# Last pair of a fused FFT convolution and spectral mixer: ten rooms for Z, W and a second block of Z read at other ticks

## The chip, the cores and the metric

One core of one Trainium2 chip. The metric is the device time of one execution in microseconds. Engines are named as in the profile: PE (matmul), PEld (its weight loads), DVE, ACT, POOL and SP. POOL and SP also issue DMAs, each on a queue of its own; each takes its instructions in order, so an instruction that waits holds up all that follow it on that engine.

## The reference

Two layers over x (8 batches, 5696 positions, 128 channels): a long convolution with h by FFT, and a spectral mixer on its result.

```python
def _attn_ref(x, h):
    B, S, D = x.shape
    L = 2 * S
    Xf = np.fft.rfft(x, n=L, axis=1)
    Hf = np.fft.rfft(h, n=L, axis=0)
    return np.fft.irfft(Xf * Hf[None], n=L, axis=1)[:, :S, :]

def _moe_ref(x, w_r, w_i, w_ch):          # n_modes = 64
    X = np.fft.rfft(x, axis=1)
    Xr, Xi = X.real[:, :n_modes], X.imag[:, :n_modes]
    Yr = einsum('bmd,mde->bme', Xr, w_r) - einsum('bmd,mde->bme', Xi, w_i)
    Yi = einsum('bmd,mde->bme', Xr, w_i) + einsum('bmd,mde->bme', Xi, w_r)
    y = np.fft.irfft(Yr + 1j * Yi, n=S, axis=1)       # other modes 0
    u = x + y
    return u + np.maximum(u @ w_ch, 0.0)
```

## The kernel before

The transform of length 11392 is done as matmuls in steps, on two batches (a pair, g = 0 to 3) at a time. For each pair:

- **First step** (`a_tile`): 32 tiles bring `Xin` through `F` into `As`.
- **Ticks** (`tick(g_, t)`): 90 frequency classes are taken four at a time, in 23 ticks (NT = 23) and 3 more to drain the pipeline. Tick t does the second transform step for its classes (`As` with `M`), the products with the filter `Hs` on DVE (tile `U`, three buffers, token `("u", t % 3)`), two ticks later the first inverse step (`U` with `Wc`), whose result ACT evicts as block s = t - 2 of Z into a room (`Zs`, `Zt`), and SP writes to the scratch `zscr` in DRAM. One tick after that PE multiplies the block with `G`, which gathers the 64 modes that the mixer needs.

A room may be filled again when its block has been written to `zscr` and read by PE. Rooms 0 to 5 are `Zs`; rooms 6 to 9 (`Zt`) lie in memory behind `G`. The last pair uses 8 rooms (`NZS`), so that block s goes into room s % 8. The memory of rooms 8 and 9 is used for `Id`, the identity of the transposes, and for `Y`, the mixer's result. `ZY` names the tokens of rooms 8 and 9, `ZX` those of rooms 6 and 7.

After the last pair's ticks comes the **output stage**: PE starts inverse sums of pair 0 (`u_z`), mixes the modes with `W` (64 times two matmuls), the result is evicted as `Y`, transposed on PE against `Id` (line 785), evicted as `C`, and then every output tile (`u_tile`) is the sum of `ZT` blocks times `S4a` and `S4b` and of `C` times `IBs`. `ZT0` to `ZT4` are five buffers for blocks of Z read back from `zscr` (16 positions of a pair each, four blocks to a pair), in two parts, a and b. When a block's tiles are done, SP loads a later block into the buffer. `o_tile` does the last matmul, with `w_ch`, and SP writes the output.

What the output stage needs is read during the last pair's ticks, by POOL, from a table by tick (`early`), each with a wait (`pace`) for that tick's product on DVE: `W` in four pieces, `S4a`, `S4b`, `IBs`, `ZT` blocks (`load_zt`) and memsets of the unused partitions of part b (`clear_zt`). Such a load may start when the memory that it takes is free: `W` lies over `Xin`, `S4b` over the first part of `As`, ZT buffers over `As`, `Hs`, `M` and `G`. `SLACK` is a further wait, for the first 15 blocks (0 to 14) of the last pair to be written to `zscr`. After the loop follow `load_wi` (two loads of 32 KB) and the remaining ZT blocks, without `pace`.

A recorder puts down every operation with what it reads and writes, and derives the waits; an operation with `after=` waits for the writers and readers of the tokens named. The semaphores of DMAs come from rings: the ring "z" of Z's writes has 8, and a DMA waits for the one that had its semaphore before.

Of the kernel before, what the change touches and what calls it, by code (L numbers as in the profile page):

```python
# [4 lines left out]
P = 128  # L5
# [118 lines left out]
def bass_long_conv_fft__then__afno_spectral_mix_kernel(nc, x, h, moe_w_r, moe_w_i, moe_w_ch, out):  # L124
# [8 lines left out]
    NP = B // 2  # L133
    KT = 4
    NT = (NK + KT - 1) // KT
# [15 lines left out]
    c, s = np.cos(th), np.sin(th)  # L151
# [35 lines left out]
    def const(name, a):  # L187
        return nc.inline_tensor(np.ascontiguousarray(a.astype(np.float16)), name=name)
# [3 lines left out]
    c_w = const("cW", np.concatenate([w1, w2, np.eye(P)], axis=1))  # L192
# [5 lines left out]
    zs = nc.dram_tensor("zscr", [NP * NK * P, 2 * D], F16, kind="Internal")  # L198
# [7 lines left out]
    def at(name, cols, dt, off):  # L206
        return nc.alloc_sbuf_tensor_at(name, [P, cols], dt, offset=off)

    def take(nbytes):
        off = (cur[0] + 31) // 32 * 32  # L210
        cur[0] = off + nbytes
        assert cur[0] <= end, (cur[0], end)
        return off
# [10 lines left out]
    a_h = take(2 * HW * 2)  # L224
# [2 lines left out]
    g_sb = at("G", GW, F16, a_g)  # L227
    ah_sb = at("Ah", HW, F16, a_g)
    NU, NXS, NZ, NZX = 3, 2, 6, 10
    NZS = [NZ] + [NZX] * (NP - 2) + [8]  # L230
    NZL = NZS[-1]
    a_st = take((2 * NU + NXS + NZ) * 2048)
    h_in = at("Hin", J * D, F16, a_st)
    DH = D // 2
# [19 lines left out]
    NC = 5  # L254
    ZP = ZB * 2 * D
    a_h2, a_xt = a_h + HW * 2, a_x + 4 * S + 2 * B * P
    a_as1, a_m2 = a_as + 2 * S, a_m + 4 * S
    zt_off = [(a_as1, a_as1 + 2 * ZP), (a_as1 + 4 * ZP, a_as1 + 6 * ZP), (a_h, a_h2), (a_h + 2 * ZP, a_h2 + 2 * ZP),
              (a_m2, a_g)]
    assert 2 * S + 8 * ZP <= AW * 2  # L260
    zt = [[at(f"ZT{i}{'ab'[p_]}", ZP, F16, zt_off[i][p_]) for p_ in range(2)] for i in range(NC)]
# [18 lines left out]
    id_sb = at("Id", P, F16, r_off[1])  # L280
# [9 lines left out]
        return bass.AP(ps, p0 * 4096 + bank * 512 + off, [[4096, n]] + [list(d) for d in dims])  # L290

    R = Recorder(nc)
    for name, n in (("c", 16), ("x", 26), ("z", 8), ("w", 16), ("t", 10), ("s", 8), ("o", 12), ("p", 16), ("q", 10)):
        R.ring(name, n)

    def bank(i):
        return ("bank", i)
# [3 lines left out]
    def evac(dst, src, reads, writes, scale=None, eng=None, after=()):  # L301
        e = eng
        if e is None:
            turn[0] ^= 1
            e = "scalar" if turn[0] else "vector"
        if e == "scalar":
            if scale is None:
                R.add(e, lambda h_: h_.copy(dst, src), reads, writes, after=after)  # L308
            else:
                R.add(e, lambda h_: h_.activation(dst, src, COPY, scale=scale), reads, writes, after=after)  # L310
        elif scale is None:
            R.add(e, lambda h_: h_.tensor_copy(dst, src), reads, writes, after=after)  # L312
        else:
            R.add(e, lambda h_: h_.tensor_scalar_mul(dst, src, scale), reads, writes, after=after)  # L314

    def dma(eng, dst, src, ring, reads=(), writes=(), after=()):
        R.add(eng, lambda h_: h_.dma_start(dst, src), reads, writes, ring=ring, after=after)  # L317
# [6 lines left out]
    def once(key, toks):  # L324
        if key in first:
            return []
        first[key] = 1
        return list(toks)
# [3 lines left out]
    def turns(name, items):  # L332
        i = ring2.get(name, 0)
        ring2[name] = i + 1
        return items[i % len(items)]
# [87 lines left out]
    for j in range(16):  # L423
        t = turns("h", [0, 2, 4])
# [11 lines left out]
        if j % 2:  # L436
            i = j // 2 % 2 * XC + j // 4
# [4 lines left out]
    AST = [("as", j) for j in range(33)]  # L442
# [40 lines left out]
    def load_w(i):  # L483
        w = 2 * M * D // 4
        dma("gpsimd", w_sb[:, i * w:(i + 1) * w], bass.AP(wd, i * w, [[2 * M * D, P], [1, w]]),
            "p", WD, [("w", i)] + (XIN if i == 0 else []), after=pace)

    H_ALL = [("h", t, 0) for t in range(NT)] + [("h", t, 1, p0) for t in range(NT) for p0 in (0, J)]
    U_ALL = [("u", i) for i in range(NU)] + [("xs", i) for i in range(NXS)] + \
            [("zs", i, b) for i in range(NZ) for b in range(2)]  # L490
    M_ALL = [("m", i) for i in range(MP)]
    G_ALL = [("g", i) for i in range(NG)]
    WT = [("w", i) for i in range(4)]
    ZY = [("zs", i, b) for i in range(NZL, NZX) for b in range(2)]
    ZX = [("zs", i, b) for i in range(NZ, NZL) for b in range(2)]
    zt_old = [(AST, AST), (AST, AST), (H_ALL, H_ALL), (H_ALL, H_ALL), (M_ALL[3:6], G_ALL)]

    def load_zt(i, eng="sync", more=()):
        g_, c_ = divmod(i, J // ZB)
        for part, (p0, r0, n) in enumerate(((0, 0, P), (PB, P, RB))):  # L500
            old = list(once(("zt", i % NC, part), zt_old[i % NC][part])) + list(more) + pace
            dma(eng, bass.AP(zt[i % NC][part], p0 * ZP, [[ZP, n], [1, ZP]]),
                bass.AP(zs, (g_ * 2 * NK + r0) * J * 256 + c_ * ZB * 256, [[J * 256, n], [1, ZP]]),
                "q" if eng == "gpsimd" else "t", [("zd", g_, s_) for s_ in range(NT)], [("zt", i % NC, part)], after=old)

    def clear_zt(i):
        z32 = zt[i][1][0:PB, :].bitcast(U32)
        R.add("gpsimd", lambda e: e.memset(z32, 0), (), [("zt0", i)], after=list(zt_old[i][1]) + pace)

    def load_ib():  # L510
        dma("gpsimd", ib_sb[:, 0:SH], c_ib.ap(), "p", (), [("ib", 0)], after=M_ALL[0:2] + pace)
# [10 lines left out]
    def load_s4(part):  # L522
        n = PB + RB if part else P
        dma("gpsimd", s4_sb[part][0:n, 0:SH], bass.AP(c_s4, part * SH, [[2 * SH, n], [1, SH]]), "p", (),
            [("s4", part, 0)], after=pace + (AST if part else M_ALL[1:4]))

    V, A = "vector", "scalar"
    border = {NT - 1: [(0, 0, V)], NT: [(1, 2, V), (2, 0, V)], NT + 1: [(3, 2, A), (4, 0, V)], NT + 2: [(5, 2, V)]}
    early = {0: lambda: load_id(), 1: lambda: load_w(0), 3: lambda: load_w(1), 6: lambda: load_w(2), 8: lambda: load_w(3),
             12: lambda: load_s4(1), 16: lambda: load_s4(0),  # L530
             14: lambda: clear_zt(0),
             15: lambda: load_zt(0, "gpsimd"),
             NT - 2: lambda: (load_ib(), load_zt(1, "gpsimd", SLACK), load_zt(2, "gpsimd"), clear_zt(1), clear_zt(2))}
    pace = []
    SLACK = [("zd", NP - 1, s_) for s_ in range(NT - NZL)]

    def load_id():
        dma("gpsimd", id_sb[:, :], bass.AP(c_w, 2 * P, [[3 * P, P], [1, P]]), "p", (), [("id",)], after=ZY)

    def load_wi():  # L540
        dma("gpsimd", wi_sb[:, P:2 * P], bass.AP(c_w, 2 * P, [[3 * P, P], [1, P]]), "p", (), [("i16",)], after=M_ALL[5:6])
# [2 lines left out]
    def keep(n, b0):  # L544
        for i in range(n):
            mm(pv(b0 + i % 2, 0, [[1, 2 * NK]]), f1_sb[:, 0:P], f1_sb[:, :], True, True, [("f1",)], [bank(b0 + i % 2)])
# [66 lines left out]
    def zroom(g_, s_):  # L613
        return (s_ - 2 * NZ) % NZX if g_ == 0 and s_ >= 2 * NZ else s_ % NZS[g_]

# [69 lines left out]
            filter_tick((j - 11) // 3, [h_, h_ + 1])  # L685
    keep(16, turns("s", FOUR))
    for g_ in range(NP):
        for t in range(NT + LM):
            tick(g_, t)
            if g_ == 0 and t < 2:  # L690
                keep(8, 4)
            assert g_ + 1 < NP or not wp
            if g_ == NP - 1 and t in early:
                pace[:] = [("u", min(t, NT - 1) % NU)]
                early[t]()
        evac(bass.AP(xt, 2 * g_ * XTW + M, [[B * XTW, P], [XTW, 2], [1, P]]), pv(MB, 0, [[P, 2], [1, P]]),
             [bank(MB)], [("xt", g_)], 1.0 / 64, eng="scalar", after=[("ag", k) for k in range(NS + 2 * XN, NK)])
        evac(bass.AP(xt, 2 * g_ * XTW, [[B * XTW, P], [XTW, 2], [1, M]]), pv(MB, M, [[P, 2], [1, M]]),
             [bank(MB)], [("xtn", g_)], -1.0 / 64, eng="vector" if g_ + 1 == NP else "scalar", after=[("ag", k) for k in range(NS + 2 * XN, NK)])
        if g_ + 1 < NP:  # L700
            for j in range(6, 32):
                a_tile(j, [(4, 6, 0, 2)[(j - 7) % 4] if j > 6 else 0], "both" if j == 31 else V if j % 2 else A)
                if j == 31:
                    keep(8, 6)
                if wp and j % 2 == 1:
                    dst, src_, ring, tok = wp.pop(0)
                    dma("gpsimd", dst, src_, ring, (), [tok], after=[("as", j)])
# [1 line left out]

    pace[:] = []  # L710
    load_wi()
    for i in range(3, NC):
        load_zt(i, "gpsimd")
        clear_zt(i)

# [63 lines left out]
    for hb in range(2):  # L779
        evac(bass.AP(y_sb, hb * 32 * B, [[2 * M * B, P], [B, 32], [M * B, 2], [1, B]]),  # L780
             pv(6 + hb, 0, [[2 * B, 32], [B, 2], [1, B]]), [bank(6 + hb)], [("y", hb)], eng="vector" if hb else "scalar",
             after=ZY)
    for b in range(B):
        bk = 6 + b // 4
        R.add("tensor", lambda e, b=b, bk=bk: e.transpose(
# [10 lines left out]
    o_cur = [0]  # L796
    o8_old = [H_ALL] * 2 + [U_ALL] + [G_ALL + ZX] * 2 + [WT] * 2
    o_old = [H_ALL] * 2 + [M_ALL[5:6], U_ALL + [("f1",)]]
# [49 lines left out]
    for g_ in range(NP):  # L848
        last = g_ == NP - 1
        order = [(c_, b) for b in range(2) for c_ in range(NCH)] if last else [(c_, b) for c_ in range(NCH) for b in range(2)]  # L850
        for n, (c_, b) in enumerate(order):
            i = NCH * g_ + c_
# [44 lines left out]
```

## Time and profile before

| | |
|---|---|
| median of 3 runs | 393.89 us (393.86 to 394.1) |
| the profiled execution | 392.87 us, of it the span of the trace 390.6 us |
| PE | 364.1 us busy, 93% of the span |
| PEld, DVE, ACT | 72%, 77%, 80% |
| POOL | 22% |
| granted TensorE clock, mean | 0.982 |
| DMA | 103.94 MB, mean 266 GB/s |
| last pair's ticks | about 221 to 263 us |
| output stage | about 263 us to the end |

Busy shares are averages over stages with different limits; matmuls overlap, so a busy PE is not PE at its peak. The chain of waits follows back from the last instruction to what released each step. A DMA's time to landing runs from its issue to its last byte's arrival. Waits for several semaphores are put down to the one that came last.

### The profile page before, as it was taken

Reading aid. Unit: us, or ns where it says so; the run is one execution under the profiler, and the core shown is the slowest. Engines: PE = TensorE matmul, PEld = TensorE weight load, DVE = VectorE, ACT = ScalarE, POOL = GpSimd, SP = SyncE. Lnnn points to the kernel's source line nnn. Section 1 sums busy time; section 2 is a strip of 40 time slices with the busy share of each in tenths; the row PEclk is TensorE's granted clock in tenths of the full one; section 3 lists DMA queues with packets and bytes.
Section 4 is the critical chain, followed back from the end, with each engine's and each line's share of the span. In section 5 each row is a group of like instructions: output and inputs, shape, how many; then the busy total and the mean of one; then the engine's idle time right before and its main releaser. Section 6 shows DMA issues by size and latency. Waiting matters only on the chain.

```text
span 390.6 us, 12485 instructions
## 1 busy us (share of the span) xinstructions
PE 364.1 (93%) x5346; PEld 281.3 (72%) x5346; DVE 301.9 (77%) x346; ACT 311.2 (80%) x489; POOL 85.6 (22%) x134
## 2 busy tenths in 40 slices
PE   7799899998989999999989899989989999999992
PEld 7698766665866667856657666658878988988871
DVE  3369889987998998989998988754437767677784
ACT  8289689997989997899997899984447676777783
POOL 8600022210643210823213210319200000000000
PEclk9899999999999999999999999996999999999998
DMA  7998569998899995999995689999999999998766
GB/s 146 178 283 337 138 126 297 274 251 251 92 135 201 238 268 169 127 136 231 245 261 111 64 264 351 298 354 379 406 388 393 414 407 412 410 399 356 305 274 273
DMA packets 87090, 103.94 MB, mean 266 GB/s; under 512 B 22824, under 2 KB 72616, under 8 KB 83564
## 3 DMA queue, kind: packets, MB, share of 16 engines
q1 hardware_dynamic: 62523, 67.73, 49.7%
q0 software_dynamic: 24512, 35.43, 43.6%
q8 instruction: 42, 0.69, 0.7%
q14 instruction: 13, 0.10, 0.1%
HBM read 70.61 MB, written 51.12 MB: 312 GB/s over the span
## 4 chain that ended last, share of the span: by engine, by line
PE 63%; DMA 15%; DVE 8%; ACT 6%; issue 3%; POOL 3%; SPq 0%; POOLq 0%; DVEq 0%
PE ps L320 63%; DMA ZT4b<-zscr 4%; DMA zscr<-Zt 3%; DMA Hs<-Hs 3%; DMA Hin<-in_h_dram 3%; DMA Xt<-in_x_dram 2%; DVE As L314 2%; DVE U L599 2%; ACT As L310 2%; DVE U L607 1%; DVE Xin L361 1%; ACT UT L308 1%; ACT Zs L308 1%; DVE Hs L312 1%; ACT Xs L308 1%
## 5 line engine op out<-in xcount | busy, mean ns | idle before, releaser
L607 DVE TENSOR_TENSOR U<-Xs,Hs 128x2048 f16<-128x2048 f16 (+1 forms) x73 | 86.9, 1192 | 15.1 <-ACT Xs L308 11.0
L320 PE MATMUL ps<-U,Wc 128*128 128x512 f16 (+1 forms) x368 | 94.0, 376 | 1.3 <-DVE U L607 0.8
L308 ACT CAST Xs<-ps 128x1024 f16<-128x1024 f32 (+1 forms) x77 | 74.7, 974 | 11.9 <-PE ps L320 6.8
L308 ACT CAST Zs<-ps 128x512 f16<-128x512 f32 (+1 forms) x134 | 70.6, 595 | 2.7 <-PE ps L320 2.4
L832 DVE TENSOR_TENSOR O<-ps,R 128x512 f32<-128x512 f32 x81 | 52.5, 685 | 19.8 <-ACT R L831 12.5
L831 ACT ACTIVATE R<-ps 128x512 f32<-128x512 f32 x96 | 50.9, 572 | 16.3 <-PE ps L320 15.8
L314 DVE TENSOR_SCALAR As<-ps 128x720 f16<-128x720 f32 x70 | 57.7, 884 | 5.4 <-PE ps L320 4.8
L320 PE MATMUL ps<-F,Xin 128*128 128x180 f16 x512 | 53.7, 249 | 3.6 <-DVE Xin L361 2.3
L320 PE MATMUL ps<-As,M 64*128 64x128 f16 x1440 | 50.5, 217 | 3.5 <-DVE U L599 2.9
L320 PEld LDWEIGHTS ps<-F,Xin 128*128 128x128 f16 x512 | 44.4, 155 | 12.1 <-DVE Xin L361 2.8
L320 PE MATMUL ps<-WI,UT 128*128 128x256 f16 x360 | 51.8, 279 | 0.5 <-DVE O L832 0.4
L320 PEld LDWEIGHTS ps<-U,Wc 128*128 128x128 f16 x368 | 28.7, 97 | 30.3 <-ACT Zs L308 4.4
L310 ACT ACTIVATE As<-ps 128x720 f16<-128x720 f32 (+1 forms) x61 | 45.7, 770 | 5.7 <-PE ps L320 4.3
L317 POOL DMA_DIRECT2D Xt<-in_x_dram x48 | 26.0, 546 | 101.0 <-PE ps L320 97.1
L320 PEld LDWEIGHTS ps<-As,M 64*128 64x128 f16 x1440 | 40.6, 94 | 9.9 <-DVE U L599 3.6
L308 ACT CAST UT<-ps 128x712 f16<-128x712 f32 x40 | 30.0, 752 | 18.7 <-PE ps L320 17.7
L320 PEld LDWEIGHTS ps<-WI,UT 128*128 128x128 f16 x360 | 39.3, 152 | 4.2 <-issue 1.9
L320 PE MATMUL ps<-IBs,C 128*128 128x356 f16 x128 | 40.5, 326 | 0.6
L320 PEld LDWEIGHTS ps<-G,Zs 128*128 128x128 f16 x524 | 26.6, 96 | 14.9 <-ACT Zs L308 2.2
L607 DVE TENSOR_TENSOR U<-ps,Hs 128x2048 f16<-128x2048 f32 x15 | 34.3, 2283 | 0.0
L320 PE MATMUL ps<-G,Zs 128*128 128x128 f16 (+2 forms) x524 | 33.0, 192 | 0.1
L312 DVE CAST UT<-ps 128x712 f16<-128x712 f32 x24 | 21.4, 890 | 11.0 <-PE ps L320 11.0
(87 smaller groups left out, 509.8 us busy)
## 6 DMA issues: line engine op xcount, KB each, us to landing
out_dram<-O SPq DMA_DIRECT2D x39, 512.0 KB, 8.7
zscr<-Zs SPq DMA_DIRECT2D x64, 256.0 KB, 7.4
Xt<-in_x_dram POOLq DMA_DIRECT2D x24, 320.0 KB, 7.3
zscr<-Zt SPq DMA_DIRECT2D x24, 256.0 KB, 7.3
W<-wscr POOLq DMA_DIRECT2D x4, 1024.0 KB, 9.1
M<-cM POOLq DMA_DIRECT2D x5, 720.0 KB, 20.6
ZT0a<-zscr SPq DMA_DIRECT2D x3, 1024.0 KB, 13.1
Hs<-Hs SPq DMA_DIRECT2D x44, 64.0 KB, 6.3
```

Source lines behind the costliest of these rows:

```text
L308: R.add(e, lambda h_: h_.copy(dst, src), reads, writes, after=after)
L310: R.add(e, lambda h_: h_.activation(dst, src, COPY, scale=scale), reads, writes, after=after)
L312: R.add(e, lambda h_: h_.tensor_copy(dst, src), reads, writes, after=after)
L314: R.add(e, lambda h_: h_.tensor_scalar_mul(dst, src, scale), reads, writes, after=after)
L317: R.add(eng, lambda h_: h_.dma_start(dst, src), reads, writes, ring=ring, after=after)
L320: R.add("tensor", lambda h_: h_.matmul(o, l, r, start=st, stop=sp), reads, writes)
L361: R.add("vector", lambda e: e.tensor_copy(bass.AP(x_sb, i * XN * XS, [[XW, NQ], [XS, XN], [1, D]]), src), list(toks) + XZ, [("xin", i)])
L599: R.add("vector", lambda e, b=b, s_=s_: e.tensor_tensor(bass.AP(u_s[i], b * 512, [[2048, P], [1024, 2], [1, n * D]]), s_, hv, MULT), [tok, ...
L607: R.add("vector", lambda e: e.tensor_tensor(uv, src, hv, MULT), bk + [("h", t, 0), ("h", t, 1, 0), ("h", t, 1, J)], [("u", i)])
L831: R.add("scalar", lambda e: e.activation(rv, src_r, RELU), bk, [("r", i % NR)], after=once(("r", i % NR), G_ALL + XTT + [("y", 0), ("y", 1 ...
L832: R.add("vector", lambda e: e.tensor_tensor(ov, src_u, rv, ADD), bk + [("r", i % NR)], [key + (h_,)], after=once(key, old))
```

## The change

In the last pair Z gets ten rooms, as in the pairs before it, and the ring "z" ten semaphores. `ZX` now names rooms 6 to 9; `ZY` is gone. `W`'s first two pieces are issued ahead of the last pair's first tick, without `pace`; the other two at ticks 3 and 5 instead of 6 and 8, `S4b` at 8 instead of 12, `IBs` at 18 instead of 21. `ZT0` now lies over the first part of `Hs` and is read at tick 11 instead of 15; `ZT1` takes `ZT0`'s former place over `As` and is read at tick 15; at tick 21 `ZT2` and `ZT3` are read instead of `ZT1` and `ZT2`; only `ZT4` is left for after the loop. `Id` is loaded by SP at tick 25, after the last write of Z, instead of by POOL at tick 0; it and `Y`'s evictions now wait for rooms 6 to 9.

```diff
-    NZS = [NZ] + [NZX] * (NP - 2) + [8]
-    NZL = NZS[-1]
+    NZS = [NZ] + [NZX] * (NP - 1)
...
-    zt_off = [(a_as1, a_as1 + 2 * ZP), (a_as1 + 4 * ZP, a_as1 + 6 * ZP), (a_h, a_h2), (a_h + 2 * ZP, a_h2 + 2 * ZP),
+    zt_off = [(a_h, a_h2), (a_as1, a_as1 + 2 * ZP), (a_as1 + 4 * ZP, a_as1 + 6 * ZP), (a_h + 2 * ZP, a_h2 + 2 * ZP),
               (a_m2, a_g)]
...
-... ("z", 8), ...
+... ("z", 10), ...
...
-    ZY = [("zs", i, b) for i in range(NZL, NZX) for b in range(2)]
-    ZX = [("zs", i, b) for i in range(NZ, NZL) for b in range(2)]
-    zt_old = [(AST, AST), (AST, AST), (H_ALL, H_ALL), (H_ALL, H_ALL), (M_ALL[3:6], G_ALL)]
+    ZX = [("zs", i, b) for i in range(NZ, NZX) for b in range(2)]
+    zt_old = [(H_ALL, H_ALL), (AST, AST), (AST, AST), (H_ALL, H_ALL), (M_ALL[3:6], G_ALL)]
...
-    early = {0: lambda: load_id(), 1: lambda: load_w(0), 3: lambda: load_w(1), 6: lambda: load_w(2), 8: lambda: load_w(3),
-             12: lambda: load_s4(1), 16: lambda: load_s4(0),
-             14: lambda: clear_zt(0),
-             15: lambda: load_zt(0, "gpsimd"),
-             NT - 2: lambda: (load_ib(), load_zt(1, "gpsimd", SLACK), load_zt(2, "gpsimd"), clear_zt(1), clear_zt(2))}
+    early = {3: lambda: load_w(2), 5: lambda: load_w(3), 8: lambda: load_s4(1),
+             10: lambda: clear_zt(0),
+             11: lambda: load_zt(0, "gpsimd"),
+             14: lambda: clear_zt(1),
+             15: lambda: load_zt(1, "gpsimd"),
+             16: lambda: load_s4(0),
+             18: lambda: load_ib(),
+             NT - 2: lambda: (load_zt(2, "gpsimd", SLACK), load_zt(3, "gpsimd"), clear_zt(2), clear_zt(3)),
+             NT + 2: lambda: load_id()}
     pace = []
-    SLACK = [("zd", NP - 1, s_) for s_ in range(NT - NZL)]
+    SLACK = [("zd", NP - 1, s_) for s_ in range(NT - 8)]

     def load_id():
-        dma("gpsimd", id_sb[:, :], bass.AP(c_w, 2 * P, [[3 * P, P], [1, P]]), "p", (), [("id",)], after=ZY)
+        dma("sync", id_sb[:, :], bass.AP(c_w, 2 * P, [[3 * P, P], [1, P]]), "c", (), [("id",)], after=ZX)
...
     for g_ in range(NP):
+        if g_ == NP - 1:
+            load_w(0)
+            load_w(1)
         for t in range(NT + LM):
             tick(g_, t)
...
-    for i in range(3, NC):
+    for i in range(4, NC):
         load_zt(i, "gpsimd")
         clear_zt(i)
...
         evac(bass.AP(y_sb, ...), ..., [("y", hb)], eng="vector" if hb else "scalar",
-             after=ZY)
+             after=ZX)
```

More of the change, by code (lines that the diff above doesn't have):

```diff
@@ L292, in bass_long_conv_fft__then__afno_spectral_mix_kernel @@
     R = Recorder(nc)
-    for name, n in (("c", 16), ("x", 26), ("z", 8), ("w", 16), ("t", 10), ("s", 8), ("o", 12), ("p", 16), ("q", 10)):
+    for name, n in (("c", 16), ("x", 26), ("z", 10), ("w", 16), ("t", 10), ("s", 8), ("o", 12), ("p", 16), ("q", 10)):
         R.ring(name, n)
```

## The prediction

> **What bounds the kernel now.** I read the page's chain first, then the chain of waits from 218 to 305 us (the last pair's ticks and the start of the output stage), then the timelines of PE, ACT and DVE there, and last the DMA issues in narrow windows. Blocks of Z are numbered 0 to 22 by their tick in the last pair.
>
> ```profile
> PE 63%; DMA 15%; DVE 8%; ACT 6%; issue 3%; POOL 3%; SPq 0%; POOLq 0%; DVEq 0%
> ```
>
> PE holds the end; DMA holds it in a few places. Two of them lie in the stretch that the change touches (columns: start us, us, what):
>
> ```profile
> 223.63 20.23 PE ps L320 x318
> ...
> 250.16 11.91 DMA zscr<-Zt
> ...
> 267.02 1.74 POOLq L105
> 268.77 1.01 POOL WI L317 x2
> ...
> 273.48 15.12 DMA ZT4b<-zscr
> 288.59 0.05 issue
> 288.64 12.47 PE ps L320 x182
> ```
>
> Block 14 is written from 250.16 and lands at 262.07. POOL waits for it (SLACK), issues four Z loads, clears and WI, and the last, ZT4b, lands at 288.59, where PE goes on. What PE itself lost is less than the chain's DMA shares. The timeline of PE (start, us, engine, line, idle before in brackets):
>
> ```profile
> 262.86 0.58 PE L320 MATMUL ps<-G,Zt 128*128 128x4 f16 x4 [0.91 <-ACT Zt L308]
> ...
> 269.84 1.05 PE L785 MATMUL ps<-Id,Y 128*128 128x128 f16 x8 [0.23 <-issue]
> ...
> 288.64 0.21 PE L320 MATMUL ps<-S4b,ZT4b 84*128 84x89 f16 x1 [1.83 <-DMA ZT4b<-zscr]
> ```
>
> The first gap, 0.91 us, is block 22 waiting for its Z room (8 rooms: that of block 14). The last, 1.83 us, is ZT4b. Between them stand the transposes of Y with Id at 269.84, which waited for nothing but work on PE, ACT and DVE.
>
> The third thing to see is how slowly Z's writes land. Three windows of DMA issues: block 13, alone at 249 us; block 19, issued at 259.27; blocks 21 and 22 beside POOL's Z loads (KB each, us from issue to landing).
>
> ```profile
> zscr<-Zs SPq DMA_DIRECT2D x1, 256.0 KB, 5.1
> ```
>
> ```profile
> zscr<-Zs SPq DMA_DIRECT2D x1, 256.0 KB, 8.4
> ```
>
> ```profile
> ZT1a<-zscr POOLq DMA_DIRECT2D x1, 1024.0 KB, 9.7
> ...
> zscr<-Zs SPq DMA_DIRECT2D x1, 256.0 KB, 17.6
> zscr<-Zt SPq DMA_DIRECT2D x1, 128.0 KB, 20.1
> ```
>
> POOL moved 1024 KB in 9.7 us while SP needed 20.1 us for 128 KB issued at 264.31: it landed at 284.4. The trace's packet records show why: from 254 to 258 us POOL's queue moved 187 packets of 5.9 and 8.2 KB, and SP's 237 of 512 B. They take turns packet by packet, so SP runs at a tenth of its speed (59 packets per us; 1231 in the two us from 260, when POOL's queue was nearly empty). Whatever stands on SP's queue behind Z's writes crawls while POOL reads Z.
>
> **The change, part by part.** The sum is made against the profiled execution, 392.87 us (span 390.6 and 2.27 around it); the median, 393.89, is 1.0 more, which I add at the end.
>
> *Ten rooms, ring z of ten.* Block 22 then takes block 12's room; block 12 was issued at 247.3 and landed by 253.1. The 0.91 us goes. In pairs 1 and 2 the ring of 8 made no PE wait, so nothing comes there.
>
> *W's first pieces ahead of the ticks.* The last wscr piece landed at 220.74, so W0 goes at about 221.3 in place of 225.28, W1 at 221.8 in place of 228.43. DMA stood still from 222 to 226 (0 GB/s by windows), so this costs nothing and moves 2 MB out of the ticks. W is used from 264.4 and landed by 246.0: no gain by itself. W2, W3 and S4b follow two to four ticks sooner, likewise unneeded so early; they fill what W0 and W1 left, so at 250 us the queues stand about as before (from 226 to 252 us POOL moved 4.7 MB; now about 4.8: W2 and W3 2.1, S4b 0.5, a Z block 1.5, the rest of W1 0.7). The POOL memset of 1.8 us moves too; beside one at 247.3 DVE's product took 2.29 us against 2.28 elsewhere: nothing.
>
> *Z blocks.* ZT0 at tick 11 (about 242.9), ZT1 at tick 15 (249.9, where ZT0 was), S4a behind it, IBs at tick 18 (254.5 instead of 259.62), ZT2 and ZT3 after SLACK, ZT4 after the loop. Behind SLACK stand 3 blocks of 1440 KB in place of 4. While POOL alone has the engines' time it moves 0.35 MB/us (packet records of 253 to 258), so 4.2 us for each block of 1.47 MB. Even if the first starts at 266.5 (below), three end near 279 and ZT4b lands near 280, against 286.6 when PE wants it: the 1.83 us goes too. Sum so far: -0.91 - 1.83 = -2.74.
>
> *Id and Y.* This is the part that decides. Rooms 8 and 9 were free in the last pair, so Id was read at 216.44 (4.5 us) and Y's evictions waited for PE alone. With ten rooms, rooms 6 to 9 hold blocks 16 to 19, and both Id's load and Y's evictions now wait until all four are written to zscr. Block 19 landed at 267.65; Y's evictions ran at 266.81 (ACT) and 269.05 (DVE), with behind them the evictions of C and U. That alone costs 0 to 2 us if block 19 lands as before. But it lands later if anything: ZT1, S4a and IBs (2908 KB) lie on POOL's queue from 250 to 261, where ZT0 and S4a were 2174 KB. Block 14 starves until they are through, so SLACK opens at 262 to 264.2 (736 KB at 0.35 is 2.1 us), and blocks 15 to 19 have only the time until ZT2's first packet, about 2.3 us later, undisturbed.
>
> Id is issued by SP after that wait, and on its queue behind blocks 20, 21 and 22. PE stops at the transposes, in order, until Id lands; ACT and DVE have C's evictions and IBs' reflection behind them; on SP stand the reloads of ZT0 and the later blocks, which wait for the first output tiles anyway. Bounds for the landing: at the best 267.65 + 4.5 (the Id row) = 272.1; at the worst block 22's own landing of before, 284.4, shortened by one Z block of POOL's (4.2), lengthened by SLACK's 2.1 less the missing IBs' 2.1 behind it, plus half of the 4.0 us that block 22 took after block 21 (Id has 128 packets, it 256): 282.2. The WI rows, 32 KB of the same form in POOL's queue, took 9.1 and 8.9 us; from 267.65 that is 276.7, with nothing of Z ahead. I take 278.0: block 22 with POOL's queue shorter is the nearest row, but less of Z is left when ZT2 starts, as IBs no longer runs from 262 to 266.
>
> Transposes at 278.0 in place of 269.84: +8.16. After them the work is the same, and ZT4b no longer stops it: -1.83 (the 0.91 lies before the wait and is swallowed). Net +6.3, 399.2 in the profile, 400.2 as median. PE's clock: 0.50 from 268 to 274 in the windows, after the thin work from 262. The new wait is longer than that, so the clock is half when work resumes; before, PE worked some 4.5 us of half clock from the transposes on. I put the difference at 0, with 1.5 us either way.
>
> The Trainium skill (TensorE: Matmul & The Clock Gate, "The HAM clock gate") says that the clock halves after an idle window of about 3.4 us and comes back after one busy window; the two 3.4-us windows of half clock here agree. By it the resumed work could lose up to 1.7 us per window, which is inside the 1.5 either way.
>
> **Rivals.**
> *Not slower.* SP's queue empties before ZT2 starts, Id lands early. It decides at 269.84 + 1.83 = 271.7, where the wait eats what ZT4b gives: a landing over 0.8 us earlier makes the kernel faster, down to 392.87 - 2.74 + 1.02 = 391.2 when nobody waits. For it: SP moved 600 packets per us at 260 to 262, so 3 us undisturbed carry 3.5 blocks. Against: block 19 itself landed at 267.65, and 4.5 us more is too late already.
> The Trainium skill (DMA: Bandwidth & Descriptors, "Queues, rings and completion order") would speak for this rival: queues take turns by packets of some 9 to 17 descriptors, so a turn of SP's would carry as much as one of POOL's and Z's writes would not starve. The trace disagrees: 232 against 237 packets, 128 KB in 20.1 us.
>
> *Starved to the end.* If block 14 is through before tick 21, SLACK opens at once, ZT2 and ZT3 follow IBs without a gap, and blocks 15 to 19 starve too; Y waits for block 19 and Id for POOL's last packet, 282 to 284: +12.2 to +14.2, less 1.83, that is 404 to 406.
>
> *A short wait.* Id at 272.5 to 274: 394.7 to 396.
>
> *The change does not reach its aim:* ZT4b late all the same. Then PE has waited for Id long before, and it costs nothing more; only under the first rival would it take back up to 1.8.
>
> **How the numbers follow.** Forecast (Id between 274 and 282, 396 to 404) 0.53; starved to the end 0.15; short wait 0.10; not slower (Id before 272.5) 0.22, of which 0.05 within 0.8 us of 393.89 (0.2%, about what a measurement of this kernel tells from no change) and 0.17 faster. Slower: 0.53 + 0.15 + 0.10 = 0.78. The range takes in most of the first rival and the lower half of the starved case: 391.5 to 405. The forecast's own range is 396 to 404.
>
> **What would show it.** Right: in the chain, a DMA Id<-cW of SP's some 8 to 12 us long; the transposes of L785 idle for 6 to 11 us before them; Y's evictions released by a zscr write; no gap at the last G,Zt or Zs product near 262; ZT4b released by nothing. W0 issued near 221. Wrong: transposes before 271.7; or PE idle within the ticks, which would mean that rooms still ran out.

## The result and the profile after

| | before | after |
|---|---|---|
| median | 393.14 us (388.19 to 394.1, 6 runs) | 401.47 us (399.8 to 402.03, 6 runs) |
| profiled execution, span | 392.87 us, 390.6 us | 401.64 us, 399.5 us |
| transposes of Y start | 269.84 us | 280.43 us |
| granted TensorE clock, mean | 0.982 | 0.964 |

The ratio is 1.025, with a 95% interval from 1.0207 to 1.0293: slower. A ratio leaves out runs that lie over 1.5% above the fastest of their kernel, so it can differ from that of the medians.

The page's chain, as shares of the span: DMA has fallen from 15% to 11%, PE has risen by six points.

```profile
PE 69%; DMA 11%; DVE 8%; ACT 6%; issue 3%; POOL 1%; SPq 0%; DVEq 0%; POOLq 0%
```

Read by shares alone that looks better. The chain of waits in the last pair shows what has gone and what has come (start us, us, what):

```profile
222.90 33.33 PE ps L319 x524
...
258.94 17.39 DMA zscr<-Zt
276.33 0.02 issue
276.35 3.94 DMA Id<-cW
280.30 0.14 issue
280.43 1.05 PE ps L790 x8
281.48 28.56 PE ps L319 x432
```

The chain now stays on PE for 33 us of the ticks, and PE's timeline has no gap of over 0.2 us from 222.9 us to the wait for `Id`, so the room's wait is gone. It stays on PE for 28.6 us after the transposes, through the first use of ZT4b at 297.56: that wait is gone too (ZT4b landed at 278.4). Between the two stands a new piece: the write of block 19, issued at 258.94, lands at 276.33, only then SP issues Id, and Id lands at 280.30. On PE it is one gap (idle in brackets):

```profile
280.43 1.05 PE L790 MATMUL ps<-Id,Y 128*128 128x128 f16 x8 [12.67 <-DMA Id<-cW]
```

The waits from 255 to 300 us show that Y's two evictions stood for the same reason, ACT's and DVE's (us in total, times, longest):

```profile
PE ps L790 <- DMA Id<-cW: 12.7, 1, 12.7
ACT Y L307 <- DMA zscr<-Zt: 11.8, 1, 11.8
DVE Y L311 <- DMA zscr<-Zt: 10.9, 1, 10.9
```

The sum nearly closes. The transposes stand 10.59 us later, and without ZT4b's wait what follows should be 1.83 us shorter, together 8.76. The spans differ by 8.91, so what follows is 1.69 shorter, 0.14 less than that. The profiled executions, some 2 us longer than their spans, differ by 401.64 - 392.87 = 8.77; that this meets 8.76 is partly chance.

### The profile page after: what moved, and what is told of

Same layout as the page of the kernel before. It is cut to its first block, busy times and chain, and to the rows that moved or that the text cites. A ratio compares the mean times of both kernels' runs of the same rounds, so it can differ in the third digit from the quotient of the medians.

```text
span 399.5 us, 12468 instructions
## 1 busy us (share of the span) xinstructions
PE 362.9 (91%) x5346; PEld 280.5 (70%) x5346; DVE 302.9 (76%) x346; ACT 310.8 (78%) x489; POOL 83.4 (21%) x133
## 4 chain that ended last, share of the span: by engine, by line
PE 69%; DMA 11%; DVE 8%; ACT 6%; issue 3%; POOL 1%; SPq 0%; DVEq 0%; POOLq 0%
PE ps L319 69%; DMA zscr<-Zt 4%; DMA Hin<-in_h_dram 3%; DVE As L313 2%; DMA Xt<-in_x_dram 2%; DVE U L601 2%; ACT As L309 2%; DMA Hs<-Hs 1%; ACT R L836 1%; DVE Xin L360 1%; DMA Id<-cW 1%; ACT UT L307 1%; DVE Hs L311 1%; DVE U L609 1%; ACT Zs L307 1%
## 5 line engine op out<-in xcount | busy, mean ns | idle before, releaser
L307 ACT CAST Zs<-ps 128x512 f16<-128x512 f32 (+1 forms) x128 | 67.0, 594 | 1.7 <-PE ps L319 1.7
L319 PEld LDWEIGHTS ps<-G,Zs 128*128 128x128 f16 x496 | 25.2, 96 | 14.1 <-ACT Zs L307 2.0
L307 ACT CAST Zt<-ps 128x512 f16<-128x512 f32 x56 | 30.6, 622 | 2.0 <-PE ps L319 2.0
L319 PE MATMUL ps<-G,Zs 128*128 128x2 f16 (+2 forms) x496 | 31.3, 192 | 0.1
```

The costliest lines, as they stand in the source:

```text
L319: R.add("tensor", lambda h_: h_.matmul(o, l, r, start=st, stop=sp), reads, writes)
```

## The experiments

Theory: PE waits for Id, and Id's landing hangs on SP's queue of Z writes, which crawls while POOL's queue has large packets. Three rivals: the loads put into the ticks cost by themselves; the wait for the rooms alone, not the queue, makes the loss; Y's wait, not Id's.

**Nothing waits for the rooms (e_free).** Ten rooms and all loads of the changed kernel; Id ahead of the ticks by POOL into free bytes, Y over U0.

```diff
-    y_sb = at("Y", 2 * B * M, F16, r_off[0])
+    y_sb = at("Y", 2 * B * M, F16, a_st)
-    id_sb = at("Id", P, F16, r_off[1])
+    id_sb = at("Id", P, F16, a_x + 33024)
-             NT + 2: lambda: load_id()}
-        dma("sync", id_sb[:, :], ..., "c", (), [("id",)], after=ZX)
+        dma("gpsimd", id_sb[:, :], ..., "p", (), [("id",)], after=XIN)
         if g_ == NP - 1:
+            load_id()
             load_w(0)
...  # Y's evictions: after=[("u", 0)]; R's first use waits for ZX, UT2's for Y
```

> The changed kernel with ten rooms and all its loads as they are, but Id read by POOL ahead of the last pair's ticks into 256 free bytes behind W, and Y laid over the product buffer U0, so that neither waits for rooms 6 to 9. Theory (the loss is PE's wait for Id, which comes from the writes of blocks 16 to 19): PE's 12.7 us idle ahead of the transposes goes, the transposes stand near 268 to 270 us, the profile near 389 to 391 and the time 1.5 to 3 us under the kernel before, since the waits of 0.91 and 1.83 us are gone too. Rival A (the loads put into the ticks cost by themselves, through contention): 397 or more still. Rival B (the half clock from 265 to 286 us, not the wait, carries a good part): 394 to 396.

Measured: 389.32 us (388.64 to 390.78, 12 runs) beside 392.41 of the kernel before (388.07 to 396.58, 35 runs), ratio 0.9958, interval 0.9928 to 0.9989. The same place on PE:

```profile
269.67 1.05 PE L790 MATMUL ps<-Id,Y 128*128 128x128 f16 x8 [0.23 <-issue]
```

The wait is gone and with it the whole loss, and neither of the two old waits has come back. This version is clearly faster than the changed kernel, and by 0.4% than the kernel before, whose fastest runs are as fast (388.07). Blocks 21 and 22 still landed only at 278.1 and 282.2 there: writes that starve cost nothing when nobody waits for them.

**The loads without the rooms (e_loads).** The changed kernel's loads; 8 rooms, ring of 8, Id and Y as before.

```diff
-    NZS = [NZ] + [NZX] * (NP - 1)
+    NZS = [NZ] + [NZX] * (NP - 2) + [8]
-    ("z", 10)
+    ("z", 8)
...  # Id by POOL at tick 0 and Y's evictions, both after rooms 8 and 9
```

> The changed kernel's loads (W's first two pieces ahead of the ticks, ZT0 at tick 11, ZT1 at tick 15, IBs at tick 18, ZT4 alone after the loop) with the rooms, the ring, Id and Y of the kernel before (8 rooms, ring of 8, Id by POOL at tick 0, Y free of rooms 6 and 7). Theory: no wait for Id; block 22's room is free in time since block 14 landed at 256.6 in the changed kernel; ZT4b in time: 390 to 392 us, as with Id and Y freed under ten rooms. Rival A (the loads cost by themselves): 397 or more. Rival D (eight rooms stop the ticks when the writes starve): a gap of several us in front of blocks 20 to 22, 394 to 400.

Measured: 390.16 us (387.72 to 393.56, 10 runs), ratio 0.9971, interval 0.9926 to 1.0017. The transposes on PE:

```profile
268.94 1.05 PE L790 MATMUL ps<-Id,Y 128*128 128x128 f16 x8 [0.23 <-issue]
```

The loads by themselves show no cost, and no gap stood in the ticks, even with blocks 18 to 22 landing from 274 to 281. So with eight rooms, too, the wait of 0.91 us for block 22's room is gone, as block 14 landed at 258.98, and ZT4b (278.62, used at 286.08) is in time: in this profile the loads alone remove both waits, and the two further rooms add nothing. The gain over the kernel before is not told from none.

**The rooms without the loads (e_rooms).** The kernel before with ten rooms, ring of ten, and Id and Y as in the change; its loads as they were.

> The kernel before with ten rooms, the ring of ten, Id by SP at tick 25 and Y's and Id's wait for rooms 6 to 9; all other loads as before (W at ticks 1 to 8, ZT0 at tick 15, ZT1 to ZT4 behind SLACK). Theory: block 19 lands near 267.7 as before, so Y waits at most 1 us, but Id stands behind blocks 20 to 22, which landed at 284.4 before beside four blocks of Z on POOL's queue: Id at 283 to 287, the transposes 13 to 17 us late, 404 to 409 us. Rival (the earlier loads are what makes the wait): 391 to 395.

Measured: 406.93 us (404.36 to 408.57), ratio 1.0336, interval 1.0265 to 1.0407. In the timeline of PE, then the DMA issue of Id (KB, us to landing):

```profile
286.98 1.05 PE L784 MATMUL ps<-Id,Y 128*128 128x128 f16 x8 [16.87 <-DMA Id<-cW]
```

```profile
Id<-cW SPq DMA_DIRECT2D x1, 32.0 KB, 17.5
```

As forecast, block 19 landed at 269.3 and Y waited little; Id, issued at 269.31, needed 17.5 us behind blocks 20 to 22. So the rooms' part of the change costs 13 to 14 us, and the loads' part, with which POOL's queue is through 8 us sooner (ZT4b at 278.4 instead of 286.5), takes 5 to 6 us of that back (401.39 for the whole change on the same chip, below).

**Id on SP's queue without any wait for rooms (e_sp).** As e_free, but SP issues Id at tick 25.

```diff
+             NT + 2: lambda: load_id()}
-        dma("gpsimd", id_sb[:, :], ..., "p", (), [("id",)], after=XIN)
+        dma("sync", id_sb[:, :], ..., "c", (), [("id",)], after=XIN)
         if g_ == NP - 1:
-            load_id()
             load_w(0)
```

> As e_free (Id in free memory, Y over U0, neither waits for rooms 6 to 9), but Id is issued by SP at tick 25 behind the last write of Z, as in the changed kernel. Theory (the place on SP's queue is enough): Id is issued when block 22's write has been and lands behind blocks 21 and 22, at 279 to 283; the transposes wait for it, 399 to 402 us. Rival (the wait for the rooms made the loss): SP issues Id near 265 and it lands by 270, 389 to 392 us.

Measured: 400.92 us (399.81 to 402.62), ratio 1.0193, interval 1.0129 to 1.0257. Y was evicted at 264.4 and 266.9, without a wait for a room. SP issued Id at 265.14; the DMA issue, and PE:

```profile
Id<-cW SPq DMA_DIRECT2D x1, 32.0 KB, 15.7
```

```profile
280.93 1.04 PE L790 MATMUL ps<-Id,Y 128*128 128x128 f16 x8 [13.47 <-DMA Id<-cW]
```

The place on the queue is enough: 32 KB took 15.7 us. e_free differs in this alone, in the queue that carries Id and the time of its issue, so some 11 us hang on these two (400.92 beside 393.01 of the kernel before, 389.32 beside 392.41). That it is not the late issue alone shows in the same run: the two loads of WI, 32 KB of the same form, were issued by POOL still later, at 268.96 and 269.50, and took 7.2 and 7.0 us.

**Id alone freed (e_id).** Id as in e_free; Y over rooms 8 and 9, waiting for rooms 6 to 9.

> The changed kernel with Id alone freed: read by POOL ahead of the ticks into 256 free bytes; Y stays over rooms 8 and 9 and waits for blocks 16 to 19. Theory: block 19 still lands near 276.3, Y's evictions run there, the transposes some 0.7 us later at 277.1, where the changed kernel has them at 280.43: 3.3 us come back, 398 us. Rival (what the prediction put most weight on: Id's place on SP's queue behind blocks 20 to 22): the wait goes nearly whole, 391 to 393. Rival A (contention by the loads): 401.

Measured: 391.62 us, but spread from 387.73 to 400.3 over 10 runs (394.9, 398.75 and 400.3 among them); the ratio is 0.9972, interval 0.9916 to 1.0027. In the profiled run block 19 had landed at 267.65, not 276.3 (ACT's timeline):

```profile
267.72 0.59 ACT L307 CAST Y<-ps 128x512 f16<-128x512 f32 x1 [2.07 <-DMA zscr<-Zt]
```

My expectation missed. Block 14 was caught behind ZT1, S4a and IBs and landed at 263.96; SLACK opened only then, and between the last packet of IBs and the first of ZT2 POOL's queue moved nothing for 2.6 us, in which SP moved 1600 packets of Z: blocks 15 to 19 landed. In the changed kernel's profile block 14 had landed at 256.56, ZT2 was issued at 259.12, that pause was 0.3 us long (221 packets), and block 19 starved. Which way it goes differs between runs, and what decides where block 14 lands was not tested.

**The way without a pause, with Id freed (e_id_open).** As e_id, with SLACK over blocks 0 to 12.

```diff
-    SLACK = [("zd", NP - 1, s_) for s_ in range(NT - 8)]
+    SLACK = [("zd", NP - 1, s_) for s_ in range(NT - 10)]
```

> As e_id (Id read by POOL ahead of the ticks into free memory, Y over rooms 8 and 9), but SLACK waits for blocks 0 to 12 only, so that it is open at tick 21 however fast the DMAs are and ZT2 and ZT3 follow IBs without a gap. Theory: blocks 17 to 19 starve every time, block 19 lands near 275 to 277, Y's evictions wait for it some 8 to 10 us, transposes near 277: 396 to 399 us in nearly every run. Rival (Y's wait is a matter of the DMA's speed in a run, not of SLACK's opening): 388 to 393 in most runs, as e_id.

Measured: 400.71 us (400.04, 401.38, 403.89 and one of 394.33). In the profiled run block 19 landed at 280.17, later than I had said (ACT, then PE):

```profile
280.24 0.59 ACT L307 CAST Y<-ps 128x512 f16<-128x512 f32 x1 [13.70 <-DMA zscr<-Zt]
```

```profile
281.04 1.05 PE L790 MATMUL ps<-Id,Y 128*128 128x128 f16 x8 [11.39 <-ACT Y L307]
```

So Y's wait by itself can cost as much as Id's, when POOL leaves no pause. That would account for the long runs of e_id, but they were not traced. I had expected 396 to 399 in nearly every run; three of the four runs were longer and one shorter.

**The changed kernel again (after_again).**

> The changed kernel unaltered, on the chip of the kernels beside it. Where Id alone was freed, the ticks went one of two ways: block 14 lands ahead of ZT1's reading, SLACK opens at once and blocks 17 to 22 starve to 274 to 280; or block 14 is caught behind ZT1, S4a and IBs and lands near 264, SLACK opens then and blocks 15 to 19 land by 268, 21 and 22 near 277 and 281. Theory (Id waits on SP for block 19 and stands behind 20 to 22): both ways end alike, Id lands at 279 to 283, 399 to 403 us, ratio 1.02 to 1.03. Rival (the loss came from the first way alone, by Y's wait): on a chip that goes the second way the loss is gone, 389 to 393.

Measured: 401.39 us (398.57 to 403.9), ratio 1.0199, interval 1.0114 to 1.0284. This time block 19 landed at 268.01, and Y was evicted there (ACT, then PE, then the DMA issue of Id):

```profile
268.08 0.58 ACT L307 CAST Y<-ps 128x512 f16<-128x512 f32 x1 [2.69 <-DMA zscr<-Zt]
```

```profile
279.96 1.04 PE L790 MATMUL ps<-Id,Y 128*128 128x128 f16 x8 [11.71 <-DMA Id<-cW]
```

```profile
Id<-cW SPq DMA_DIRECT2D x1, 32.0 KB, 11.8
```

Yet Id, issued at 268.03, landed at 279.83 behind blocks 20 to 22, and the time is the same. This run also shows that block 14 alone does not decide how block 19 fares: it landed at 255.78, as early as in the profile under the result, but the pause before ZT2's first packet was 0.7 us instead of 0.3, and block 19 got through.

This is the clearest sign: whether Id is issued at 265.14 (e_sp), 268.03 (here) or 276.35 (the profile under the result), it lands at 280.80, 279.83 or 280.30, within 2 us after ZT4b (280.45, 278.87, 278.40). In e_rooms too: ZT4b 286.50, Id 286.85. In these four runs Id lands when POOL's large packets are through. It is no rule for all that stands on SP's queue: the last write of Z landed 4.2, 2.2 and 3.8 us ahead of ZT4b in the kernel before, e_free and e_id.

**POOL pauses (e_slack).** The changed kernel; ZT2 and all behind it wait for blocks 0 to 19.

```diff
-    SLACK = [("zd", NP - 1, s_) for s_ in range(NT - 8)]
+    SLACK = [("zd", NP - 1, s_) for s_ in range(NT - 3)]
```

> The changed kernel with one number changed: ZT2, ZT3 and all behind them on POOL's queue wait until blocks 0 to 19 (not 0 to 14) are written. Theory (Z's writes starve only because POOL's queue never runs empty): POOL's queue is empty from about 261.5 us, blocks 15 to 19 land by 264 to 267, Y's evictions run without a wait of over 2 us, Id lands at 267 to 272, and ZT4b lands by 284, ahead of its use: 390 to 395 us. Rival A: 399 or more. Rival C (SP's writes are slow by themselves, whatever POOL does): block 19 lands near 276 all the same, and the ZT loads come later still: 403 to 410.

Measured: 394.13 us (391.36 to 400.23, 10 runs), ratio 1.0072, interval 1.0027 to 1.0117. Blocks 15 to 22 landed at 0.4 to 0.8 us from each other, Id 2.1 us after its issue, and PE waited 0.76 us:

```profile
272.07 1.04 PE L790 MATMUL ps<-Id,Y 128*128 128x128 f16 x8 [0.76 <-DMA Id<-cW]
```

The pause takes away most of the loss, which shows that SP's writes are slow here only beside POOL's reads. It does not pay: ZT4b landed at 291.3, not by 284 as I had expected, and PE waited 1.31 us for it.

## Why the prediction was right, and where it was not

The direction and the place were right: the new wait of PE ahead of the transposes, for Id, outweighs the two waits removed. e_sp and after_again show the mechanism that was forecast, Id behind Z's last writes on SP's queue while POOL reads. The forecast was 400.2 us, the measured median 401.47. That the first profile, the one under the result, fits the number too is in part luck: it took another of the ways that I had listed, *starved to the end*, which I had priced 2 to 5 us too high.

- *Ten rooms*: the 0.91 us went, as said, and PE had no gap in the ticks. But e_loads, with eight rooms, had none either: the rooms were not needed for it.
- *W's pieces*: that they bring nothing by themselves was not tested alone; all loads together showed no cost (e_loads). W0 went at 219.95, not 221.3, as the last wscr piece had landed at 219.38.
- *Z blocks*: -1.83 us, right. I had ZT4b near 280; it landed at 278.4, and at 284.4 in e_free, where PE, not held up by Id, used it at 286.84.
- *SLACK opens at 262 to 264.2*: wrong for both profiles of the changed kernel, near for e_free, e_id and e_sp (264.41, 263.96, 262.75). In the first profile block 14 landed at 256.56, SLACK was open at tick 21, and ZT2 was issued at 259.12. SP's backlog was a little shorter than I had carried over: block 13 landed at 252.45, not 253.95, and block 14 slipped through beside ZT1, whose part a landed at 256.49. This is the way of the rival *starved to the end*; I had given it 404 to 406 us.
- *Y waits 0 to 2 us*: wrong for the first profile, where ACT waited 11.8 us for block 19 and Id, issued only then, took 3.94 us and held PE for the last 3.3 (Y's evictions ended at 277.10); the sign that I had named, an Id of 8 to 12 us, is missing there. In after_again Y waited 2.7 us and Id took 11.8.
- *Id at 278.0*: mis-sized, 280.30 measured (delay 10.46 us of landing against the transposes of before, not 8.16). I had built it from block 22's landing and SP's remaining packets. In the four runs in which PE waited long for Id it landed 0.35 to 1.9 us after ZT4b, so the end of POOL's queue was the nearer row. I had that end near 280 in the step before and did not use it here. The same slip made the rival too dear: starving ends with POOL's queue at 278.4, not at 282 to 284.
- *Clock*: I had put the difference at 0, with 1.5 us either way. Half clock lasted from 265.2 to 285.7 instead of 267.5 to 274.4, but for 12.7 us of that PE stood still; after the transposes began it lasted 5.3 us instead of 4.5, and the sum above leaves 0.14 us for it. Two things I had wrong beside it. The 1.7 us per window does not lie inside 1.5 either way. And the trace agrees with the idle and busy windows of the Trainium skill (TensorE: Matmul & The Clock Gate, "The HAM clock gate") in their length alone, 6.83 us for two of them: in the 3.41 us before the clock fell in the kernel before, PE was busy for 3.21, so it was not an idle window.
- *Packets in turns*: that SP moves about one packet for one of POOL's is borne out; in e_sp, from 266 to 279 us, SP's queue moved 879 and POOL's 664. But this does not speak against the turns of 9 to 17 descriptors of the Trainium skill (DMA: Bandwidth & Descriptors, "Queues, rings and completion order"), as I had it: turns of as many descriptors on both queues give about equal numbers as well. My mistake was to take equal numbers for equal bytes, where SP's packets have 512 B and POOL's up to 8 KB.

The rival *not slower* needed Id before 271.7. Of the runs that load Id behind Z on SP's queue only e_slack came near it (271.94), with a pause that no version of the forecast had.

## What to carry to other kernels

A small load that the critical engine will need must not stand behind bulk writes on one queue while another queue reads in large packets: here it cost some 11 us, and the same 32 KB issued over 40 us earlier on the other queue cost nothing. Before a buffer is shared with a ring of rooms, ask which DMA last reads each room and when that one lands; two more rooms bought nothing that the earlier loads did not give by themselves (e_loads), and turned a free patch of memory into a wait of 12.7 us. And where two transfers race for one queue, look at the spread of the runs: a median of 391.62 hid runs of 400.

## What the runs showed of the hardware

The 16-bit tensor_scalar on DVE that reflects `S4a` or `IBs` waits when it meets a memset on POOL. Reflecting S4a took 0.93 us in the kernel before, where no memset ran at its start; in the changed kernel, where two memsets ran from 261.21 to 264.77, it took 3.17 us from 262.34 (DVE, then POOL):

```profile
262.34 3.17 DVE L518 TENSOR_SCALAR S4a<-S4a,SG 128x2759 f16<-128x2759 f16 x1
```

```profile
261.21 1.82 POOL L506 MEMSET ZT2b<- 32x2048 uint32 x1
262.95 1.82 POOL L506 MEMSET ZT3b<- 32x2048 uint32 x1
```

It ended 0.74 us after the second memset, less than its own 0.93; why it is less is not shown. In all ten profiles the reflections that began inside a memset took 2.1 to 3.3 us and ended 0.74 us after the last memset that they met; the others took 0.93 to 0.98. The Trainium skill (SBUF — State Buffer, "Terms") calls the pair of ports that DVE and GpSimd share an exclusive lock held for the full instruction; these rows agree in that the reflection waited to the memset's end, and show that it waited through a second memset too. It cost nothing here, as PE did not wait for S4a's reflected half.

Issuing a DMA can itself hold SP up. In the changed kernel issuing block 22's write took from 265.64 to 273.20, 7.6 us. In all ten profiles a write of Z in the last pair took 0.36 us to issue when at most one earlier write had not yet landed, and between 0.36 and 7.9 us when three or more had not. A limit on what the queue holds would explain it, but which limit is not shown: some issues with four writes on the way took 0.36 us.
